# A long convolution by two-step Fourier transforms: length 4,096 split 64 by 32 in place of 128 by 16

## The chip, the core and the metric

The kernel runs on one core of a Trainium2 chip. The core has a matrix engine (TensorE, "PE" in the profile; its weight loads are "PEld"), VectorE (DVE), ScalarE (ACT), GpSimd (POOL) and SyncE (SP), which here issues all data transfers. Matmul results land in a separate memory, PSUM, and are copied ("evicted") to the on-chip memory SBUF by ScalarE or VectorE. The metric is the device time of one execution in microseconds; the median of three runs of the kernel before is 180.91 us (180.76 to 182.53).

## What is computed

Two independent results stand side by side in the output, for a sequence of 2,048 and 576 channels. A: keys `k` are filtered by a four-tap shift filter and multiplied by `v`; the product `kv` is convolved along the sequence with a filter `ssm_k` of 2,048 taps per channel; `kv` times a per-channel constant is added, and all is multiplied by `q`. B: a linear-attention block on `x`.

```python
# A
for t in range(ks):                                   # ks = 4
    k_shift = k_shift + k_pad[:, t:t + S, :] * shift_k[:, ks - 1 - t][None, None, :]
kv = k_shift * v
y_f = rfft(pad(kv, 2 * S)) * rfft(pad(ssm_k, 2 * S))  # shortened
y = irfft(y_f)[:S] + kv * ssm_D
a = q * y
# B, H = 32 heads of 18
phi = lambda t: jnp.where(t > 0, t + 1, jnp.exp(t)) + 1e-6
pq, pk = phi(q), phi(k)                               # q, k, v from x @ wqkv
kv = jnp.einsum("bhsd,bhse->bhde", pk, v)
num = jnp.einsum("bhqd,bhde->bhqe", pq, kv)
den = jnp.einsum("bhqd,bhd->bhq", pq, pk.sum(s)) + 1e-6
b = (num / den).reshape(B, S, D) @ wo
```

(`pad`, `rfft`, `irfft` and the last lines are shortened.)

## The kernel before, in words

The transform of the convolution is done with matmuls in two steps. Sequence position is written 16 a + b, with a on the 128 partitions and b from 0 to 15.

For each of five groups of channels (`ci`, four of 128 and one of 64) these units run; the number in brackets is the line of the profile:

- `hl`, `hT` [L445]: load the filter, 16 transposes put position a on partitions, one eviction of 2,048 columns, and the constant `ssm_D` is added to tap 0 on VectorE.
- `cv` 0 to 3 [L429 to L435]: the shift filter and the product with `v` on VectorE, in place in `v`.
- `h1`, `u1` (function `s1`) [L462]: first step, a matmul with the 128x128 table `G[ri][:, b, :]` for each b and real or imaginary part; four units for each group, each of eight matmuls into one PSUM tile and one eviction into `Ch` or `Cu`.
- `ht`, `ut` [L469]: two transposing transfers for each group (one for the last group) from `C` to `Ct`.
- `h2`, `u2` (function `s2`) [L485]: second step with the small table `W0` on tiles of 64 rows by 32 columns of the array, eight matmuls and one eviction for each unit, two units (x = 0, 1) for each half (`hf`), into `T` (filter) or `SU` (signal).
- `pX`, `pT` [L495, L497]: the products of the two spectra on VectorE.
- `i1` [L509]: inverse of the second step on 64-row tiles, 32 matmuls and one eviction into `V` for each unit, two units (z) for each half.
- `i2` [L522, L523]: inverse of the first step with `F`, the transposes of `G` (`FT`, L531); 16 matmuls and, on VectorE, the product with `q` straight from PSUM [L524].
- `st`: store.

Block B has the units `xT`, `xU` (transposes of `x`), `k` (16, L400), `q` (12, L409), `G` (5, L562), `kv`, `den`, `M` (L592), `bc` (L625), `o` (16, L634), each with one PSUM tile and one to two evictions or point operations.

The order of everything is written out by hand as a list of units (`ORDER`), one stream that every engine follows for its own part. A trailing `A` or `D` says whether ScalarE or VectorE evicts. PSUM is a ring of four tiles of two banks (`bufs=4`, tag `big`); every unit takes its tile from there in the order of the list. All transfers are issued on SP's queue, so one that waits holds up those behind it. The tables are made on the chip at the start: `io` and `iw` (GpSimd index patterns), `ix` (VectorE, index for the 128-point table), `iv` and `wk` (GpSimd: phases and a mask for the 16-point tables), `sin` and `sw` (ScalarE sines), `W` (VectorE), `id` (the identity for transposes), and `wu` (40 matmuls on zeros at the start).

Of the kernel before, what the change touches and what calls it, by code (L numbers as in the profile page):

```python
# [8 lines left out]
FP32 = mybir.dt.float32  # L9
BF = mybir.dt.bfloat16  # L10
# [6 lines left out]
S = 2048  # L17
# [13 lines left out]
wm io wu.0 wu.40 hl.0 xl.0 id ix.0 ix.1 xl.1 sin.1 ls hT.0.D one xT.0.D iw sin.0 FT.1.D iv wk xU.0.A lw.1  # L31
h1.0.0.0.A xT.1.D h1.0.0.1.D h1.0.1.1.D Wj sw W k.3 lw.0 xU.1.D kl.0 k.0 q.0.1 cv.0.0 h1.0.1.0.A q.1.2 xl.2
cv.0.1 hl.1 q.1.0 FT.0.A ht.0.1 cv.0.2 q.0.0 hT.1.A k.7 k.1 k.2 xl.3 h2.0.1.0.A hl.2 vl.0 cv.0.3 h1.1.0.0.A
k.6 h2.0.1.1.A q.1.1 ht.0.0 k.5 cv.1.0 u1.0.0.0.A k.4 u1.0.1.0.A u1.0.1.1.A xT.2.D u1.0.0.1.A h1.1.1.1.D q.0.2
h2.0.0.0.A xU.2.D ql.0 cv.1.1 h1.1.0.1.A xT.3.A h2.0.0.1.A cv.1.2 q.2.1 h1.1.1.0.A ut.0.0 cv.1.3 xU.3.A q.2.0
ut.0.1 u2.0.0.0.A u2.0.0.1.A hl.3 q.3.0 k.11 u2.0.1.0.A k.10 q.2.2 u2.0.1.1.A ht.1.0 h2.1.0.0.A hT.2.D
u1.1.0.0.D vl.2 ht.1.1 u1.1.1.0.A q.3.2 u1.1.1.1.A pX.0.1 u1.1.0.1.A h2.1.0.1.D k.12 h2.1.1.0.A k.14
h1.2.0.0.D h1.2.0.1.A k.9 kl.1 pT.0.1 h1.2.1.0.A h2.1.1.1.A cv.2.0 ut.1.1 k.15 k.8 ut.1.0 pX.0.0 u2.1.1.0.A
pT.0.0 vl.1 k.13 cv.2.1 h1.2.1.1.A u2.1.1.1.A q.3.1 eps kl.2 ht.2.1 u2.1.0.0.A cv.2.2 i1.0.0.0.A hc i1.0.0.1.A
i1.0.1.1.A lwv i1.0.1.0.A cv.2.3 G.2 h2.2.1.0.A cv.3.0 pX.1.1 u2.1.0.1.A cv.3.1 ht.2.0 h2.2.1.1.A hT.3.A G.1  # L40
u1.2.0.0.A hl.4 u1.2.0.1.A u1.2.1.0.D i2.0.1 es u1.2.1.1.A ut.2.0 pX.1.0 i2.0.0 h1.3.0.0.A cv.3.2 h1.3.1.0.A
G.3 pT.1.1 cv.3.3 h1.3.1.1.A h2.2.0.0.A cv.4.0 h2.2.0.1.A G.4 h1.3.0.1.A u2.2.0.0.A cv.4.1 ut.2.1 pT.1.0
cv.4.2 u2.2.0.1.A ht.3.0 G.0 lwo cv.4.3 i1.1.0.0.A u2.2.1.0.D u2.2.1.1.A i1.1.1.0.A i1.1.1.1.A pX.2.1 kv
ht.3.1 i1.1.0.1.A pX.2.0 pT.2.1 M.4 u1.3.0.0.A h2.3.0.0.A den u1.3.1.0.A u1.3.0.1.A h2.3.1.0.A i2.1.0
u1.3.1.1.A h2.3.1.1.A i2.1.1 u1.4.0.0.A u1.4.1.1.A M.3 bc.0.1 h2.3.0.1.A ql.2 ut.3.1 bc.0.0 bc.1.0 M.2
u1.4.0.1.A u1.4.1.0.A bc.3.0 M.1 M.0 ut.3.0 u2.3.1.0.A pT.2.0 hT.4.D u2.3.1.1.A bc.4.0 i1.2.0.0.A bc.2.0
ut.4.0 ql.1 i1.2.1.0.A i1.2.1.1.A u2.3.0.0.A u2.3.0.1.D pX.3.1 i1.2.0.1.A bc.3.1 h1.4.0.0.A o.5 bc.1.1 o.4
h1.4.0.1.A bc.2.1 bc.4.1 h1.4.1.0.A o.6 h1.4.1.1.D ht.4.0 i2.2.1 o.11 o.10 o.3 pT.3.1 o.13 pX.3.0 o.2 st.0
pT.3.0 h2.4.0.0.D u2.4.0.0.A u2.4.0.1.A i1.3.0.0.A i1.3.1.0.D i1.3.0.1.A h2.4.0.1.D pX.4.0 i1.3.1.1.D i2.2.0
o.12 pT.4.0 o.15 o.9 i2.3.0 o.1 i2.3.1 i1.4.0.0.D st.1 i1.4.0.1.A o.7 o.0 i2.4.1 i2.4.0 st.2 o.14 o.8  # L50
# [661 lines left out]
```

## Time and profile before

| | us |
|---|---|
| median of three runs | 180.91 |
| span of the profiled execution, first to last instruction | 178.8 |
| chain that ended last: PE 55%, DVE 24%, ACT 7%, POOL 5%, DMA 3% | |
| ACT waiting for `o_ps`, late in the run | 14.2 |
| DVE waiting for `i_ps` | 3.8 |

The rows of the groups that the change touches, with line, engine, operation, tensors, shapes and count, then busy us, mean ns of one, and idle time before them:

```
L462 PEld LDWEIGHTS <-G 128*128 128x128 bf16 x320 | 17.6, 98 | 2.7 <-issue 1.6
L509 PE MATMUL i_ps<-W,T 64*128 64x128 bf16 x288 | 16.9, 217 | 0.5 <-DVE pqT L393 0.5
L277 ACT ACTIVATE SU<-s_ps 128x1024 bf16<-128x1024 f32 x16 | 16.0, 1020 | 0.1
L277 ACT ACTIVATE Ch<-s_ps 128x1024 bf16<-128x1024 f32 x12 | 12.1, 1019 | 0.9 <-PE s_ps L462 0.9
L203 POOL TENSOR_SCALAR_AFFINE_SELECT sm<-sm 64x384 f32<-64x384 f32 x2 | 2.5, 1226 | 0.1
L218 ACT ACT_TABLE_LOAD x1 | 1.3, 1283 | 0.0
q8 instruction: 17, 0.28, 0.7%
```

A matmul's duration is its way through the array; matmuls follow each other more closely than that, so the spacing of their starts says what they cost. "64*32" is the used part of the array, rows by columns. The last row is the queue that brings instructions: packets, MB, share of 16 engines.

### The profile page before, as it was taken

How to read it: one execution, taken by the hardware profiler on the slowest of the kernel's cores; microseconds unless marked ns; L12 is line 12 of the kernel's file. 1: busy time of each engine (PE TensorE's matmuls, PEld its weight loads, DVE VectorE, ACT ScalarE, POOL GpSimd, SP SyncE). 2: the span in 40 equal slices, each digit the busy share in tenths (PEclk: the TensorE clock that was granted, in tenths of full speed). 3: DMA queues.
4: the chain of work that ended last, by engine and by line, in shares of the span. 5: the costliest groups of instructions: out<-in, count | busy, mean ns of one | idle time of the engine just before them, and what ended most of it. 6: DMA issues, size and time to landing. Idle time of an engine off the chain costs nothing.

```text
span 178.8 us, 5118 instructions
## 1 busy us (share of the span) xinstructions
PE 164.8 (92%) x2246; PEld 111.6 (62%) x2256; DVE 151.2 (85%) x174; ACT 128.7 (72%) x147; POOL 21.0 (12%) x59
## 2 busy tenths in 40 slices
PE   6996999999999999989799898998789999999991
PEld 6973575576654755575477453876557665686760
DVE  7987999999998879999949998779899789579720
ACT  3897578899998989984688257749887953754341
POOL 1189100000049810000000000000000000000000
PEclk9999999999999999999999999999999999999998
DMA  5999599973997799989722393791696937481295
GB/s 173 364 321 293 191 217 343 188 214 63 177 144 148 135 287 149 245 137 213 157 69 53 64 121 66 190 165 30 33 206 64 268 93 151 167 242 66 79 291 125
DMA packets 71208, 29.96 MB, mean 168 GB/s; under 512 B 46936, under 2 KB 70482, under 8 KB 71186
## 3 DMA queue, kind: packets, MB, share of 16 engines
q1 hardware_dynamic: 71186, 29.64, 74.0%
q8 instruction: 17, 0.28, 0.7%
q14 instruction: 5, 0.04, 0.1%
HBM read 15.48 MB, written 4.72 MB: 113 GB/s over the span
## 4 chain that ended last, share of the span: by engine, by line
PE 55%; DVE 24%; ACT 7%; POOL 5%; DMA 3%; issue 2%; SPq 1%; DVEq 0%; POOLq 0%; ACTq 0%
PE o_ps L634 11%; PE k_ps L400 7%; PE g_ps L562 7%; PE i_ps L509 6%; PE q_ps L409 6%; DVE at L432 5%; DVE at L431 5%; PE s_ps L462 5%; DMA x_sb<-in_B_x_dram 3%; PE bc_ps L625 3%; DVE pqT L393 3%; PE hT_ps L445 2%; PE s_ps L485 2%; ACT Cu L277 2%; DVE pk L393 2%
## 5 line engine op out<-in xcount | busy, mean ns | idle before, releaser
L409 PE MATMUL q_ps<-xT,wqk 128*126 128x512 bf16 (+3 forms) x100 | 23.7, 381 | 0.0
L400 PE MATMUL k_ps<-wqk,xT 128*128 128x64 bf16 (+3 forms) x154 | 21.5, 282 | 1.4 <-DVE Ch L279 0.8
L562 PE MATMUL g_ps<-pk,x_sb 128*128 128x65 bf16 (+3 forms) x156 | 20.4, 284 | 1.4 <-ACT wv_GT L566 1.1
L634 PE MATMUL o_ps<-wo_M,pqT 126*128 126x512 bf16 (+3 forms) x160 | 21.0, 286 | 0.0
L639 ACT ACTIVATE ob<-o_ps 128x576 bf16<-128x576 f32 x16 | 10.4, 652 | 14.2 <-PE o_ps L634 14.2
L462 PEld LDWEIGHTS <-G 128*128 128x128 bf16 x320 | 17.6, 98 | 2.7 <-issue 1.6
L400 PEld LDWEIGHTS <-xT 128*128 128x128 bf16 (+1 forms) x160 | 11.5, 97 | 12.3 <-issue 2.3
L277 ACT ACTIVATE V<-i_ps 128x1024 bf16<-128x1024 f32 x15 | 14.9, 1029 | 5.8 <-PE i_ps L509 5.8
L562 PEld LDWEIGHTS <-x_sb 128*128 128x128 bf16 (+1 forms) x160 | 11.0, 101 | 11.3 <-issue 1.9
L509 PE MATMUL i_ps<-W,T 64*128 64x128 bf16 x288 | 16.9, 217 | 0.5 <-DVE pqT L393 0.5
L409 PEld LDWEIGHTS <-wqk 128*126 128x126 bf16 (+3 forms) x100 | 12.4, 131 | 7.8 <-issue 1.1
L432 DVE TENSOR_TENSOR at<-at 128x2048 bf16<-128x2048 bf16 (+1 forms) x15 | 16.8, 1119 | 0.5
L634 PEld LDWEIGHTS <-pqT 126*128 126x128 bf16 (+1 forms) x160 | 10.9, 97 | 9.9
L509 PE MATMUL i_ps<-W,X 64*128 64x128 bf16 x288 | 16.8, 216 | 0.0
L431 DVE TENSOR_TENSOR at<-k,Wj 128x2048 bf16<-128x2048 bf16 (+1 forms) x15 | 16.7, 1111 | 0.1
L277 ACT ACTIVATE Cu<-s_ps 128x1024 bf16<-128x1024 f32 (+1 forms) x18 | 15.9, 928 | 0.7 <-PE s_ps L462 0.5
L277 ACT ACTIVATE SU<-s_ps 128x1024 bf16<-128x1024 f32 x16 | 16.0, 1020 | 0.1
L392 ACT ACTIVATE pqT<-q_ps,neg 126x1024 bf16<-126x1024 f32 (+1 forms) x12 | 11.6, 970 | 5.6 <-PE q_ps L409 5.6
L277 ACT ACTIVATE T<-s_ps 128x1024 bf16<-128x1024 f32 x15 | 15.3, 1026 | 0.0
L277 ACT ACTIVATE Ch<-s_ps 128x1024 bf16<-128x1024 f32 (+1 forms) x15 | 13.9, 937 | 1.1 <-PE s_ps L462 1.1
L524 DVE TENSOR_TENSOR q<-i_ps,q 128x1024 bf16<-128x1024 f32 (+1 forms) x10 | 11.0, 1109 | 4.0 <-PE i_ps L523 3.8
L392 ACT ACTIVATE pk<-k_ps,neg 128x576 bf16<-128x576 f32 x16 | 11.8, 742 | 2.6 <-PE k_ps L400 2.3
(121 smaller groups left out, 308.4 us busy)
## 6 DMA issues: line engine op xcount, KB each, us to landing
x_sb<-in_B_x_dram SPq DMA_DIRECT2D x4, 576.0 KB, 5.6
out_dram<-ob SPq DMA_DIRECT2D x16, 144.0 KB, 1.8
h_sb<-in_A_ssm_k_dram SPq DMA_DIRECT2D x4, 512.0 KB, 4.1
k<-in_A_k_dram SPq DMA_DIRECT2D x2, 1024.0 KB, 7.6
v<-in_A_v_dram SPq DMA_DIRECT2D x2, 1024.0 KB
q<-in_A_q_dram SPq DMA_DIRECT2D x2, 1024.0 KB
out_dram<-q SPq DMA_DIRECT2D x2, 1024.0 KB
wqk<-in_B_wqkv_dram SPq DMA_DIRECT2D x2, 576.0 KB, 8.9
```

What stands on the lines that cost most here:

```text
L277: nc.scalar.activation(out=out, in_=in_, func=ACT.Copy)
L392: nc.scalar.activation(out=out_ap, in_=ps_ap, func=ACT.Exp, bias=K.neg1[0:n, :])
L400: nc.tensor.matmul(ps[:, n0:n1], lhsT=xT[r // 4][0:fn, t, rr * 128:(rr + 1) * 128], rhs=wqk[0:fn, t, D + n0:D + n1], start=(t == 0), stop= ...
L409: nc.tensor.matmul(ps[0:hn, j, :], lhsT=wqk[0:fn, t, h0:h0 + hn], rhs=xT[g][0:fn, t, :], start=(t == 0), stop=(t == 4))
L431: nc.vector.tensor_tensor(out=t_, in0=kk[:, 3 - stage:19 - stage], in1=wb(stage), op=ALU.mult)
L432: nc.vector.tensor_tensor(out=a_, in0=a_, in1=t_, op=ALU.add)
L462: nc.tensor.matmul(ps[:, bi, 0:dc], lhsT=K.G[ri][:, b, :], rhs=xf(b), start=True, stop=True)
L509: nc.tensor.matmul(ps[:, r, g, :], lhsT=s[key, hf][64 * r:64 * r + 64, z, x, 128 * g:128 * g + 128], rhs=K.W[64 * r:64 * r + 64, m, :], st ...
L524: nc.vector.tensor_tensor(out=qs, in0=ps[:, :, 0:dc], in1=qs, op=ALU.mult)
L562: nc.tensor.matmul(ps[0:fn, n0:n1], lhsT=x_sb[:, r, f0:f0 + fn], rhs=pk[:, r, n0:n1], start=(r == 0), stop=(r == 15))
L634: nc.tensor.matmul(ps[:, n0:n1], lhsT=pqT[0:hn, c, r * 128:(r + 1) * 128], rhs=B['M'][0:hn, c, n0:n1], start=(c == 0), stop=(c == 4))
L639: nc.scalar.activation(out=ob, in_=ps[:, 0:D], func=ACT.Copy)
```

## The change

Position is now written 32 a + 16 h + b, with a from 0 to 63 and the half h on the two halves of the partitions, so the first step has 64 points and the second 32.

- First step: table `G` is 64 wide with real and imaginary parts side by side; two matmuls, one for each half of the partitions, on 64x128 tiles. A unit has four b and eight matmuls.
- Second step: 32x32 tiles, table `W` of 160 columns for everything small. One unit now does both x for a half: 64 matmuls, two PSUM tiles and two evictions (two letters, `AD`: the first by ScalarE, the second by VectorE).
- Inverse of the second step: 32x128 tiles, 128 matmuls of 64 columns, two PSUM tiles and two evictions for each half.
- Inverse of the first: 64x64 tiles, 64 matmuls of half the columns.
- `hT` and `FT`: 32 transposes of half the width in place of 16; `FT` also scales by 1/S.
- Small tables: index patterns by GpSimd in `io`, made together; `iv`, `wk`, `W` are gone. The index table has 1,024 columns in place of 2,048.
- Loads of `k`, `v`, `q` and the stores go by halves of the partitions.
- A new order of all units, with new letters. `sw` (sine of the small table, then setting the `Exp` table) now stands ahead of the two `sin`.
- Some tiles (`xT`, `wv_GT`, `wo_M`) are made at their first use, whichever unit that is.

```diff
+def _w32_index(tc, K):
     nc = tc.nc
     sm = K.sm
...
+    row = sm[:, 2:3].bitcast(I32)
+    nc.vector.tensor_single_scalar(out=row, in_=sm[:, 1:2].bitcast(I32), scalar=31, op=ALU.bitwise_and)
+    nc.vector.tensor_copy(out=sm[:, 3:4], in_=row)
+    K.wi = sm[:, 608:768].bitcast(I32)
+    nc.vector.scalar_tensor_tensor(out=K.wi, in0=sm[:, 288:448], scalar=sm[:, 3:4], in1=sm[:, 448:608], op0=ALU.mult,
+                                   op1=ALU.add)
+    nc.vector.tensor_single_scalar(out=K.wi, in_=K.wi, scalar=31, op=ALU.bitwise_and)
...
+def _sine32(tc, cpool, K):
...
+    K.W = cpool.tile([128, 160], BF, name="W32")
+    nc.scalar.activation(out=K.W[:], in_=K.wi, func=ACT.Sin, scale=TWO_PI / 32, bias=K.negpi[:])
     nc.scalar.activation(out=K.warm[:], in_=K.neg1[:], func=ACT.Exp)
...
-        hv = h[0:dc, :].rearrange("d (a b) -> d b a", b=16)
+        hv = h[0:dc, :].rearrange("d (a h b) -> d b h a", h=2, b=16)
         for b in range(16):
-            nc.tensor.transpose(out=ps[:, b, 0:dc], in_=hv[:, b, :], identity=K.ident[0:dc, 0:dc])
+            for g in range(2):
+                nc.tensor.transpose(out=ps[64 * g:64 * g + 64, b, 0:dc], in_=hv[:, b, g],
+                                    identity=K.ident[0:dc, 0:dc])
...
-        ps = psum.tile([128, 8, 128], FP32, name="s1_ps", tag="big")
-        for bi in range(8):
-            b = 8 * bg + bi
-            nc.tensor.matmul(ps[:, bi, 0:dc], lhsT=K.G[ri][:, b, :], rhs=xf(b), start=True, stop=True)
...
+        ps = psum.tile([128, 2, 4, 128], FP32, name="s1_ps", tag="big")
+        for bi in range(4):
+            b = 4 * bg + bi
+            for h in range(2):
+                nc.tensor.matmul(ps[:, h, bi, 0:dc].rearrange("p (f q y) -> p f q y", q=2, y=32),
+                                 lhsT=K.G[64 * h:64 * h + 64, b].rearrange("p r k -> p (r k)"),
+                                 rhs=xf(b)[64 * h:64 * h + 64].rearrange("p (q f y) -> p f q y", q=2, y=32),
+                                 start=True, stop=True)
+        evict(C[:, 0:dc, :].rearrange("p d (h g b) -> p g h d b", h=2, b=4)[:, bg],
+              ps[:, :, :, 0:dc].rearrange("p h b d -> p h d b"), eng)
...
-        ps = psum.tile([128, 2, 512], FP32, name="s2_ps", tag="big")
-        for r in range(2):
-            for j in range(2):
-                q = 32 * (2 * r + j)
-                for z in range(2):
-                    nc.tensor.matmul(ps[q:q + 32, z, :], lhsT=K.W0[64 * z:64 * z + 64, x, :],
-                                     rhs=Ct[64 * z:64 * z + 64, r, :, j, :], start=True, stop=True)
-        evict(s[dst, hf][:, :, x, :], ps[:], eng)
+        ps = [psum.tile([128, 2, 2, 256], FP32, name="s2_ps", tag="big") for _ in range(2)]
+        for x in range(2):
+            for r in range(2):
+                w = {(0, 0): 0, (1, 0): 32, (0, 1): 96, (1, 1): 0}[r, x]
+                for c in range(4):
+                    for t in range(4):
+                        nc.tensor.matmul(ps[t // 2][32 * c:32 * c + 32, t % 2, x, :],
+                                         lhsT=K.W[32 * t:32 * t + 32, w:w + 32],
+                                         rhs=Ct[32 * t:32 * t + 32, r, c], start=(r == 0), stop=(r == 1))
+        for i in range(2):
+            evict(o[:, 2 * i:2 * i + 2], ps[i][:], eng[i])
...
-        ps = psum.tile([128, 2, 4, 128], FP32, name="i1_ps", tag="big")
-        for g in range(4):
-            for n, (key, x, m) in enumerate((('T', 0, 0), ('T', 1, 1), ('X', 0, 2), ('X', 1, 2))):
-                for r in range(2):
-                    nc.tensor.matmul(ps[:, r, g, :], lhsT=s[key, hf][64 * r:64 * r + 64, z, x, 128 * g:128 * g + 128],
-                                     rhs=K.W[64 * r:64 * r + 64, m, :], start=(n == 0), stop=(n == 3))
...
+        ps = [psum.tile([128, 2, 8, 64], FP32, name="i1_ps", tag="big") for _ in range(2)]
+        for m in range(2):
+            for t in range(4):
+                for n, (key, x, w) in enumerate((('T', 0, 0), ('T', 1, 64), ('X', 0, 96), ('X', 1, 96))):
+                    for c in range(4):
+                        nc.tensor.matmul(ps[c // 2][:, c % 2, 4 * m + t, :],
+                                         lhsT=s[key, hf][32 * c:32 * c + 32, t, x, 128 * m:128 * m + 128],
+                                         rhs=K.W[32 * c:32 * c + 32, w:w + 64], start=(n == 0), stop=(n == 3))
+        for i in range(2):
+            d = 32 * hf + 16 * i
+            evict(V[:, :, d:d + 16], ps[i][:].rearrange("p c g j -> p j (c g)"), eng[i])
...
-            nc.tensor.matmul(ps[:, bi, 0:dc], lhsT=K.F[0][:, b, :], rhs=V[:, b, 0:dc], start=True, stop=False)
-            nc.tensor.matmul(ps[:, bi, 0:dc], lhsT=K.F[1][:, b, :], rhs=V[:, 16 + b, 0:dc], start=False, stop=True)
-        nc.vector.tensor_tensor(out=qs, in0=ps[:, :, 0:dc], in1=qs, op=ALU.mult)
+            for r in range(2):
+                for q in range(2):
+                    for h in range(2):
+                        nc.tensor.matmul(ps[64 * h:64 * h + 64, q, bi, 0:n],
+                                         lhsT=K.F[r][64 * q:64 * q + 64, 16 * h + b, :],
+                                         rhs=V[64 * q:64 * q + 64, 32 * r + 16 * h + b, 0:n],
+                                         start=(r == 0), stop=(r == 1))
...
+        for h in range(2):
+            nc.sync.dma_start(out=outA[h][:, :, d0:d0 + dn], in_=KV['q', gi][64 * h:64 * h + 64])
```

The new order begins and ends like this, the old one above it:

```diff
-wm io wu.0 wu.40 hl.0 xl.0 id ix.0 ix.1 xl.1 sin.1 ls hT.0.D one xT.0.D iw sin.0 FT.1.D iv wk xU.0.A lw.1
-h1.0.0.0.A xT.1.D h1.0.0.1.D h1.0.1.1.D Wj sw W k.3 lw.0 xU.1.D kl.0 k.0 q.0.1 cv.0.0 h1.0.1.0.A q.1.2 xl.2
...
-o.12 pT.4.0 o.15 o.9 i2.3.0 o.1 i2.3.1 i1.4.0.0.D st.1 i1.4.0.1.A o.7 o.0 i2.4.1 i2.4.0 st.2 o.14 o.8
+wm io wu.0 iw sw wu.40 ix.0 one xl.1 hc sin.1 ix.1 id sin.0 xT.1.D xU.1.D FT.0.D xl.0 xT.0.A xU.0.D lw.1 k.7 k.6
+lw.0 q.0.0 hl.0 q.0.2 hT.0.D ls Wj k.3 k.0 k.2 h1.0.3.A kl.0 cv.0.0 cv.0.1 h1.0.2.A k.1 q.0.1 xl.2 cv.0.2 xT.2.A
...
+o.12 o.11 pX.4.0 pT.4.0 i1.4.0.DA o.6 i2.4.0 i2.4.1 st.2 o.3 o.13
```

## The prediction

> **What bounds the kernel now.** First the page: the busy times of part 1, then the stretches by engine.
>
> ```profile
> PE 164.8 (92%) x2246; PEld 111.6 (62%) x2256; DVE 151.2 (85%) x174; ACT 128.7 (72%) x147; POOL 21.0 (12%) x59
> ```
>
> ```profile
> 0.00:20.00 20.00, 16.12 (x175) 13.55 (x177) 16.64 (x27) 13.65 (x13) 10.35 (x33) 1.00 0.98 297
> 20.00:60.00 40.00, 39.29 (x391) 25.23 (x393) 38.03 (x40) 35.49 (x39) 7.79 (x16) 1.00 0.80 172
> 140.00:179.00 39.00, 35.06 (x548) 23.15 (x542) 25.27 (x23) 19.00 (x27) 0.00 (x0) 0.98 0.58 163
> ```
>
> After length, the columns are PE, PEld, DVE, ACT, POOL. TensorE is the busiest engine throughout and VectorE is close to it until late. A busy PE is only overlapping durations, so I count its work by spacings. They come from the chain of waits (start, us, what) and the PE timeline (start, us, what):
>
> ```profile
> 38.61 0.90 PE s_ps L462 x16
> 57.63 0.56 PE s_ps L485 x16
> 141.64 1.23 PE o_ps L634 x10
> 26.18 1.00 PE hT_ps L445 x16
> ```
>
> ```profile
> 118.74 0.28 PE L509 MATMUL i_ps<-W,X 64*128 64x128 bf16 x4
> 118.85 0.28 PE L509 MATMUL i_ps<-W,T 64*128 64x128 bf16 x4
> 119.88 0.61 PE L462 MATMUL s_ps<-v,G 128*128 128x128 bf16 x8
> 120.43 0.41 PE L485 MATMUL s_ps<-Cth,W 64*32 64x512 bf16 x8
> 121.88 0.29 PE L604 MATMUL den_ps<-epsc,zsel 126*32 126x1 bf16 x20
> 122.10 1.07 PE L462 MATMUL s_ps<-v,G 128*128 128x128 bf16 x16
> ```
>
> The reader should see four prices. A full-array matmul of 128 columns takes 0.90/16 = 56 ns (L462). On half-array tiles (L509) four take 0.11 us: 28 ns each, two at once. On 64x32 tiles (L485) eight run at once, 16 of 512 columns in 0.56 us. A change of tile shape costs 0.10 us: eight of L462 at 56 ns from 119.88 end at 120.33, L485 starts at 120.43.
>
> So counted, with all other units by like rows (10 of `k` or `o` 1.23 us, 10 of `q` 2.17, a `G` 4.15), TensorE has 161 us of work in a span of 178.8. The other 17.4 are about 5 in the first 20 us (the units done by then add up to 15), 4 after the last matmul group (the last eviction and store), 8 of waits between. The median of the runs, 180.91, is 2.1 above the span; I carry that.
>
> **The change, part by part.**
>
> *Stage 1 (`h1`, `u1`).* 320 matmuls stay 320, on 64x128 tiles, two at once. Before: 256 of 128 columns at 56 ns and 64 of 64 columns at 29 (the 64-column matmuls of `o`: 1.23 less five of 217 leaves 0.15 for five) = 16.2 us. After: half, 8.1. Gain 8.1.
>
> *Stage 3 (`i1`).* Before 576 at 28 ns = 16.1. After 1,152 of 64 columns on 32x128 tiles, rounds of four on four row groups: 288 rounds. Nothing shows four row groups; the nearest row is the 64-column spacing, 29 ns for a round = 8.4. Gain 7.7; if only two overlap, 16.7 and a loss of 0.6. L604 bears on whether 64 columns are too few: its 20 one-column matmuls, in four column groups, take some 0.12 us (121.88 to 122.10 less the change of shape), 24 ns for four, so what a small matmul costs beyond its columns is paid by each tile beside the others. [...]
>
> *Stage 4 (`i2`).* Before 128 x 56 + 32 x 29 = 8.1. After 640 on 64x64 tiles, 160 rounds of four. I take 31 ns a round (64 weight columns load without the speed of the 128-column form: mean load 112 ns at 72 columns, 98 at 128) = 5.0. Gain 3.1; with two overlapping, a loss of 1.8.
>
> *Stage 2 (`h2`, `u2`).* 288 matmuls of 512 columns, eight at once, become 1,152 of 256 columns, sixteen at once: 36 rounds of 0.22 against 72 of 0.11. Nothing either way.
>
> *Transposes `hT`, `FT`.* 16 become 32 half as wide, in two column groups. The four column groups of L604 run together, so I cost this at nothing; if pairs don't overlap, 16 more at 62 ns (1.00/16) are 1.0 us for each of seven, 7 us.
>
> *Tile shapes.* Stages 1 and 4 and the transposes shared the full-array shape with `k`, `q`, `G`, `o`; now each has its own. Counted along the two orders the shape changes 99 times, 65 before: 34 x 0.10 = 3.4 us lost.
>
> TensorE: 161 - 8.1 - 7.7 - 3.1 + 3.4 = 146.
>
> *VectorE.* Evictions marked D: 15 fall to 8 (14 full ones to 7): -7 x 1.21 = -8.5. `FT` and `hT` +1 each, `xT` -2, all 1.2: nothing. Tables: before 7.6 (2.28, 1.23, 1.23, 0.70 for the index and 2.1 for the 16-point tables); after, 1,024 columns in place of 2,048 and one 160-wide table, about 4. Sum 151 - 12 = 139.
>
> *ScalarE.* +7 x 1.02 of evictions; `xT` +2, `hT` and `FT` -1 each (1.9) nothing; sines -2.4. The new order sets the `Exp` table between the sines, and a table load takes 1.28: two more, +2.6. Sum 129 + 7.4 = 136. The evictions of stages 1 and 3 now read PSUM in steps of 128 or 64 elements. `Ch` (pairs) at 1.019 and `SU` (plain) at 1.020 show no price for a pattern, so 1.02; 10% more would be 5 us.
>
> *Start.* The GpSimd tables behind `W` end the chain's first 18 us (select instructions of 1.2 us, then VectorE's 0.56), and PE idles some 2 us there. That goes. But the identity now stands behind the index tables on VectorE: GpSimd's iotas to about 2.7, tables 4, so the first transposes start near 6.9, and `FT.0` waits for the second sine: index to 6.5, two sines of 1.0, 8.6. PE reaches `k.7` near 10.7, against `k.3` at 12.1 with the transform of `h` behind it. By 10.7 it has done 7.3 us of work (the warm-up's 4.0 among it), so 3.5 are lost in front, 1.5 fewer than now; 2 more or fewer are possible.
>
> *Loads in halves.* `v`, `q` and the stores become two issues each, `k` stays at three; each SP issue took 0.3 to 0.6 us. The nine more add about 4 us on SP's queue, which waits some 80 us for transposes' inputs: nothing, and 1 us late per load where one is due just then.
>
> *Instruction supply.* PE's instructions grow from 4,514 to 8,578. The queue page has 17 instruction transfers for 17.6 blocks of 256, and each took 0.9 to 1.7 us. By the sums above seven new blocks (a whole `i1` is one) run in 0.9 to 1.3 us. I add 3 us.
>
> *Sum.* 146 + 3 + 3.5 + 4 = 156.5. VectorE (139) and ScalarE (136) now lie within 10 us of TensorE, so waits between will be no fewer than now; I take 8 as before. Span 164.5, time 167. A second way: I cut both orders into ten stretches and add, stretch by stretch, the busiest engine's work at the same prices: 170 us before, nine short of the span, and 152 after. 152 + 9 + 3 of instruction supply is 164.
>
> **The rivals.**
>
> *B, slower: TensorE's own instruction rate.* The sums need 128 instructions of `h2` in 0.45 us and 256 of `i1` in 0.93: 3.6 ns each. What the trace sustains is L509: eight in 0.11 us, 14 ns. L604 is faster, 40 in about 0.12 us, but they could have been queued behind 0.2-us matmuls. Sequencer and array stand apart: L592's wait is recorded at 118.93 and its matmul starts at 119.61, with 38 instructions between. With 38 in hand and 14 ns for the others, `h2`/`u2` lose 0.8 us x 18, `i1` 2.1 x 9, `i2` 0.76 x 10: 41 us, 208 in time. The 14 us between 167 and 181 are used up at 8 ns; mid-way, at 11, +28 gives 195. For it: nothing sustained below 14 ns is in the trace. Against: L509's 14 ns is what its 128 columns take on two tiles anyway, so it measures no limit of instructions. [...]
>
> *C, no change: PSUM evacuation.* `h2`, `u2` and `i1` now fill two of the four PSUM buffers at once and free neither until all is done: 0.45 or 0.93 us of matmuls, then two evictions of 1.02 on ScalarE. If each of the 27 units waits 0.6 us (half an eviction) for its second buffer, 16 us come back: about 181. For it: ScalarE is at 35.5 of 40 us from 20 to 60 already. Against: only 9 of these 27 follow another convolution unit directly on PE (36 of 54 before); most stand behind `k`, `q`, `G` or `o`, whose matmuls take longer than their evictions (1.23 against 0.74). [...]
>
> *D, faster still.* The waits between fall to nothing and the supply costs nothing: 146 + 3.5 + 4 + 2 = 155.5, up to 160.
>
> **How the numbers follow.** Forecast (160 to 176, around 167) 0.56; B (182 to 208, around 193, a little under mid-way) 0.24; C (176 to 184, around 180) 0.14; D 0.06. A percent, 179.1 to 182.7, is what a measurement of this kernel can tell from no change. Faster: forecast and D, and 0.05 of C: 0.67. Same: 0.07 of C and 0.01 of B: 0.08. Slower: 0.25. The range goes from 158, with half of D below, to 191, with somewhat over half of B above: 0.16 left out. The forecast's own range is 160 to 176.
>
> **What would show it.** Right: L462's successor spaced at 28 ns, a whole `i1` in about 0.95 us, a `h2` in about 0.5; TensorE's busy time down by some 15 us; VectorE near 139, ScalarE near 136. B: `i1` matmuls evenly spaced at 15 to 28 ns with no releaser, PEld idle put down to "issue". C: PE idle before `s_ps` or `i_ps` released by ScalarE, 10 us or more in sum. Wrong otherwise if the first `k` comes after 13 us, or if evictions of `C` or `V` are longer than 1.1 us.

## The result and the profile after

The changed kernel takes 212.78 us (median of 4 runs, 208.96 to 215.2) against 180.83 us for the kernel before on the same chip: ratio 1.159, 95% interval 1.150 to 1.169. Executions of one kernel fall into a faster and a slower state; the ratios and intervals here compare executions in the faster one, the medians are over all. The profiled execution took 211.94 us, its span is 210.1 us. First the page of the changed kernel: busy times, granted clock in 40 slices, two DMA queues, the shares of the chain that ended last.

```profile
PE 173.0 (82%) x4275; PEld 110.6 (53%) x4288; DVE 142.1 (68%) x164; ACT 136.7 (65%) x156; POOL 14.2 (7%) x39
...
PEclk9999999999999999859999997999985697979955
...
q1 hardware_dynamic: 71312, 29.64, 74.5%
q8 instruction: 33, 0.54, 1.1%
...
PE 59%; issue 14%; DVE 10%; DMA 9%; ACT 4%; SPq 3%; POOL 1%; ACTq 0%; POOLq 0%; DVEq 0%
```

VectorE and ScalarE stand where the sum put them (142 and 137 us; 139 and 136 were forecast). TensorE does not: its busy time rose by 8 us though its work was to fall by 15, and it stands idle more. The clock row has holes that the kernel before (the next row) lacks until its end, and "issue", time for which nothing in the profile is to blame, is now 14% of the chain; it was 2%.

```profile
PEclk9999999999999999999999999999999999999998
```

The changed kernel by stretches (length, then PE, PEld, DVE, ACT, POOL, granted clock, DMA share, GB/s):

```profile
0.00:20.00 20.00, 16.96 (x189) 13.12 (x192) 13.37 (x24) 15.60 (x16) 13.02 (x35) 1.00 0.85 239
20.00:60.00 40.00, 38.66 (x558) 24.40 (x563) 34.67 (x36) 34.10 (x39) 0.00 (x0) 1.00 0.98 161
...
140.00:180.00 40.00, 28.84 (x1037) 17.63 (x1036) 24.05 (x25) 24.69 (x33) 0.00 (x0) 0.83 0.68 123
```

Up to 60 us TensorE is as full as before. From 140 to 180 it is busy for 28.8 of 40 us at a mean clock of 0.83. What it waits for there is in the chain of waits (start, us, what), here over two units of `i1`, 256 matmuls:

```profile
150.28 0.80 PE i_ps L473 x86
151.08 3.97 issue
155.05 1.49 PE i_ps L473 x128
156.54 3.33 issue
159.88 0.77 PE i_ps L473 x39
160.65 4.91 PE o_ps L622 x20
```

TensorE breaks off in the middle of a unit, with every input there, stands for 4 us, runs 128 matmuls, and stands for 3.3 us. Counted in matmuls plus weight loads, the stops of more than 0.9 us (ten of them, later than 80 us) all lie at whole multiples of 256 from one another. Counted from one start to the next, the spacings over 0.3 us within two instructions of such a boundary add up to 27.9 us at 15 boundaries. The idle time in them is 24.2 us, at 11 boundaries; the kernel before has no idle gap over 0.3 us at one. The instruction queue (q8) has 33 transfers in place of 17. Its packets, of 16 KB each, show what ends the stops: each of the ten ends 1.3 to 1.5 us after such a packet has landed. In no trace here does a block of 256 start sooner than 1.1 us after its packet.

Behind seven of the ten stops come matmuls at half speed: `o` (L622) takes 4.91 us for 20 above, where the kernel before took 2.46. The records of the clock show 0.50 from 87.6 to 94.4 us, 128.5 to 131.9, 155.8 to 166.1, 172.9 to 176.3, 183.1 to 186.5 and from 200.2 to the end: 37.2 us, in 27.2 of which TensorE was busy.

The PE timeline between the stops (start, us, what) shows the prices of work that is not interrupted:

```profile
58.71 0.84 PE L445 MATMUL s_ps<-Ctu,W 32*32 32x256 bf16 x64
59.48 1.40 PE L353 MATMUL k_ps<-wqk,xT 128*128 128x512 bf16 x9
...
150.78 0.25 PE L473 MATMUL i_ps<-W,X 32*128 32x64 bf16 x8
150.85 0.23 PE L473 MATMUL i_ps<-W,T 32*128 32x64 bf16 x6
155.05 0.20 PE L473 MATMUL i_ps<-W,T 32*128 32x64 bf16 x2 [3.97 <-issue]
```

A `s2` of 64 has its successor 0.77 us after its start (0.45 and 0.10 for the change of shape were forecast), eight `i1` matmuls 0.06 to 0.07 us (8 ns each with their weight loads, four at once), up to the matmul where the block of instructions ends.

A ledger of the two profiled executions: TensorE busy 164.8 before and 173.0 after, its idle gaps 8.5 and 31.8. These 8.2 + 23.3 make 31.5 us; the spans differ by 31.2, since the idle time at start and end is 0.3 us shorter.

### The profile page after: what moved, and what is told of

The parts are those of the page before. It is cut to its first block, busy times and chain, and to the rows that moved or that the text cites. A ratio compares the mean times of both kernels' runs of the same rounds, so it can differ in the third digit from the quotient of the medians.

```text
span 210.1 us, 9157 instructions
## 1 busy us (share of the span) xinstructions
PE 173.0 (82%) x4275; PEld 110.6 (53%) x4288; DVE 142.1 (68%) x164; ACT 136.7 (65%) x156; POOL 14.2 (7%) x39
## 3 DMA queue, kind: packets, MB, share of 16 engines
q1 hardware_dynamic: 71312, 29.64, 74.5%
## 4 chain that ended last, share of the span: by engine, by line
PE 59%; issue 14%; DVE 10%; DMA 9%; ACT 4%; SPq 3%; POOL 1%; ACTq 0%; POOLq 0%; DVEq 0%
PE o_ps L622 11%; PE g_ps L548 10%; PE q_ps L362 6%; PE i_ps L473 6%; DMA x_sb<-in_B_x_dram 6%; PE k_ps L353 5%; PE s_ps L445 5%; PE s_ps L419 4%; PE hT_ps L399 4%; DMA wqk<-in_B_wqkv_dram 3%; PE i_ps L490 3%; SPq L319 2%; PE bc_ps L613 2%; ACT Cu L221 2%; DVE pqT L616 2%
## 5 line engine op out<-in xcount | busy, mean ns | idle before, releaser
L622 PE MATMUL o_ps<-wo_M,pqT 126*128 126x512 bf16 (+3 forms) x160 | 28.6, 344 | 0.0
L548 PE MATMUL g_ps<-pk,x_sb 128*128 128x65 bf16 (+3 forms) x156 | 22.4, 299 | 5.8 <-issue 5.7
L221 ACT ACTIVATE V<-i_ps 128x1024 bf16<-128x1024 f32 x14 | 13.8, 1024 | 13.7 <-PE i_ps L473 8.8
L221 ACT ACTIVATE Cu<-s_ps 128x1024 bf16<-128x1024 f32 (+1 forms) x19 | 17.3, 960 | 7.1 <-PE s_ps L419 3.6
L495 DVE TENSOR_TENSOR q<-i_ps,q 128x1024 bf16<-128x1024 f32 (+1 forms) x10 | 10.9, 1114 | 14.9 <-PE i_ps L490 14.8
L622 PEld LDWEIGHTS <-pqT 126*128 126x128 bf16 (+1 forms) x160 | 13.0, 113 | 15.1 <-issue 8.4
L221 ACT ACTIVATE SU<-s_ps 128x1024 bf16<-128x1024 f32 x18 | 17.4, 1023 | 2.7 <-PE s_ps L445 2.5
L473 PE MATMUL i_ps<-W,T 32*128 32x64 bf16 x576 | 11.8, 195 | 8.6 <-issue 8.4
L221 ACT ACTIVATE Ch<-s_ps 128x1024 bf16<-128x1024 f32 (+1 forms) x19 | 17.0, 936 | 0.2
L221 ACT ACTIVATE T<-s_ps 128x1024 bf16<-128x1024 f32 x16 | 15.6, 1024 | 1.5 <-PE s_ps L445 1.3
L346 DVE SCALAR_TENSOR_TENSOR pk<-pk,k_ps 128x576 bf16<-128x576 bf16 x16 | 11.9, 752 | 5.7 <-ACT pk L345 5.7
L419 PEld LDWEIGHTS <-G 64*128 64x128 bf16 x320 | 9.4, 95 | 11.7 <-issue 10.8
L552 ACT ACTIVATE wv_GT<-g_ps,ex 128x576 bf16<-128x576 f32 (+1 forms) x5 | 3.7, 739 | 17.7 <-DVE ex L551 17.7
L473 PEld LDWEIGHTS <-T 32*128 32x128 bf16 x576 | 10.1, 93 | 9.5 <-issue 9.0
```

Of the source, the lines that this page charges most:

```text
L221: nc.scalar.activation(out=out, in_=in_, func=ACT.Copy)
L346: nc.vector.scalar_tensor_tensor(out=out_ap, in0=out_ap, scalar=1.0, in1=ps_ap, op0=ALU.min, op1=ALU.max)
L419: nc.tensor.matmul(ps[:, h, bi, 0:dc].rearrange("p (f q y) -> p f q y", q=2, y=32), lhsT=K.G[64 * h:64 * h + 64, b].rearrange("p r k -> p ...
L473: nc.tensor.matmul(ps[c // 2][:, c % 2, 4 * m + t, :], lhsT=s[key, hf][32 * c:32 * c + 32, t, x, 128 * m:128 * m + 128], rhs=K.W[32 * c:32 ...
L495: nc.vector.tensor_tensor(out=qs, in0=ps[:, :, :, 0:n], in1=qs, op=ALU.mult)
L548: nc.tensor.matmul(ps[0:fn, n0:n1], lhsT=x_sb[:, r, f0:f0 + fn], rhs=pk[:, r, n0:n1], start=(r == 0), stop=(r == 15))
```

## The experiments

Theory 1: instructions reach TensorE in blocks of 256, with one block ahead, and a block that is used up faster than the next arrives stops the engine. Rivals: a cost added by each instruction; a lowest time of each instruction by itself, however dense (B's mechanism); no limit of instructions, but small tiles or late inputs. All edits are to the kernel before or to the changed kernel, as said.

| run | edit | median us | ratio to before, 95% |
|---|---|---|---|
| e1_dense | before, small matmuls halved | 198.75 | (195.63 to 200.22 us) |
| e2_wide | before, big matmuls quartered | 184.1 | 1.004 to 1.027 |
| e3_tail | before, 2,560 instructions behind its end | 212.52 | one run |
| e4_fewer | changed, `i1`, `i2` in fewer matmuls | 189.06 | 1.030 to 1.050 |
| e10_sum | changed, `i1` in 96 matmuls, not 128 | 202.2 | 1.094 to 1.116 |
| e12_sum_spaced | the same, `o` spread out | 205.07 | 1.115 to 1.135 |
| e9_pauses | before, two pauses of TensorE | 205.34 | 1.112 to 1.137 |
| e5_halves | before, transfers in halves | 184.62 | 1.006 to 1.015 |
| e6_whole | changed, transfers whole | 205.27 | 1.120 to 1.134 |
| e7_fewer_whole | changed, both of e4 and e6 | 182.13 | 0.998 to 1.008 |
| e11_flat | changed, `hT` reads adjacent columns | 207.19 | one run |
| e13_flat_too | e7 and e11 together | 181.06 | 0.993 to 1.002 |
| e14_early | e13, one transfer earlier | 180.61 | 0.987 to 0.998 |
| e8_sum | before, halves of X added first | 186.68 | 1.009 to 1.027 |

### More instructions in the kernel before: where it matters

The first run splits the matmuls of the short units, the second those of the long ones; both issue about 6,500 TensorE instructions in place of 4,514 for the same sums.

```diff
 # e1_dense: i1; the same in s2 (256 columns) and i2 (64)
+            for f in range(2):
...
-                    nc.tensor.matmul(ps[:, r, g, :], ..., rhs=K.W[64 * r:64 * r + 64, m, :], ...)
+                        nc.tensor.matmul(ps[:, r, g, 64 * f:64 * f + 64], ...,
+                                         rhs=K.W[64 * r:64 * r + 64, m, 64 * f:64 * f + 64], ...)
 # e2_wide: k; the same in q, G and o
-        for n0, n1 in ((0, 512), (512, 576)):
+        for n0, n1 in ((0, 128), (128, 256), (256, 384), (384, 512), (512, 576)):
```

> The kernel before, with the matmuls of its dense units cut in column halves: i1 and i2 into 64 columns, h2 and u2 into 256. Same sums, tiles, order and evictions; TensorE's instructions go from 4,514 to 6,498, the added ones where units are short. Theory 1 (instruction supply: a block of 256 instructions that runs in under some 4.4 us stalls TensorE until the next block is fetched): eight blocks then run in about 1.8 to 3 us, 19 us short in sum, of which two thirds show as in the changed kernel: 10 to 18 us with the slower clock after stalls, 191 to 200 us. Theory 2 (the new tile shapes or the new order are slow, not the count): array time grows by 1 to 3 us only, 181 to 184 us. Theory 3 (every instruction costs its time wherever it stands): 28 us for 4,064 more in the changed kernel is 7 ns each, so 1,984 more give 14 us, as the next run does.

> The kernel before, with the 512-column matmuls of k, q, G and o cut into four of 128: TensorE's instructions go to 6,554, nearly as many as in the run before, but the added ones stand in long units. Theory 1: only one block of 256 runs in under 4.4 us (3.8), so nothing stalls; the cut costs 2.3 ns for each of 1,020 matmuls, 2 to 3 us on TensorE: 182 to 185 us. Theory 2: the same, 182 to 185 us. Theory 3: 14 us and more, 195 us.

Nearly the same number of instructions costs 13 to 18 us in the short units (195.63 to 200.22 against 182.29 beside it) and 2 to 3 in the long ones (184.1). The waits of e1 (engine, line, what was waited for: us in total, times, longest):

```profile
PEld L511 <- issue: 8.0, 11, 1.9
PEld L568 <- issue: 6.2, 13, 2.6
PE i_ps L511 <- issue: 6.0, 5, 1.7
```

The longest wait on "issue" in e2 is 1.2 us, against 1.0 before. So it is not the number of instructions, but how many fall into a short time: a cost added by each instruction is out. A lowest time of each, B's mechanism, could give the same two results, for a quartered matmul of e2 takes 56 ns with its load (the price of L462's 128 columns), more than B's 28 for two instructions; the next run decides on that. The profiled execution of e1 also has 14.9 us at half clock, the kernel before 1.1.

### The price of a block alone

```diff
+    def small(n):
+        ps = psum.tile([128, 128], FP32, name="small_ps", tag="big")
+        for i in range(n):
+            j = i % 4
+            nc.tensor.matmul(ps[32 * j:32 * j + 32, 0:1], lhsT=K.ident[:, 0:32], rhs=K.ident[:, 0:1], ...)
...
-st.2 o.14 o.8
+st.2 o.14 o.8 sm.1280
```

> The kernel before, with 1,280 one-column matmuls on 32-column tiles added behind its last unit, where no data is loaded: ten blocks of 256 instructions whose array time is about 6 ns a pair, 0.8 us a block. Theory 1: bursts of 256 instructions with gaps at block boundaries, one block in 3 to 4.5 us, 30 to 45 us longer; if the fetch is slow only because of data transfers beside it, nearer 2.5 us a block. An even decode rate (rival B as first written) would show even spacing of 12 to 14 ns an instruction and 31 to 36 us. No limit: 8 us.

Ten blocks behind the last unit. The PE timeline of this run:

```profile
183.35 1.19 PE L659 MATMUL small_ps<-ident 128*32 128x1 bf16 x128 [2.54 <-issue]
186.81 1.18 PE L659 MATMUL small_ps<-ident 128*32 128x1 bf16 x128 [2.27 <-issue]
190.53 1.18 PE L659 MATMUL small_ps<-ident 128*32 128x1 bf16 x128 [2.54 <-issue]
193.99 1.18 PE L659 MATMUL small_ps<-ident 128*32 128x1 bf16 x128 [2.27 <-issue]
```

128 matmuls and their 128 loads run in 1.2 us (the granted clock is 0.50 there), and then TensorE waits for 2.3 to 2.5 although nothing else is left to transfer (DMA share 0.03). From block to block it is mostly 3.45 and 3.73 us in turn. In the changed kernel two blocks in a row at full clock are 3.73 us apart as well (entered at 119.4, 123.1 and 126.8 us). Not an even rate: bursts and one stop a block. The first 141 matmuls of the tail ran without a stop, over a boundary, and the next had to wait: one block stands ready ahead, no more.

The packets of q8 divide the time. In the tail, from its second stop on, a packet starts 1.0 to 1.3 us after a block is entered, takes 0.9 to 1.4 us, and the next block starts 1.2 to 1.4 us after it has landed. In the changed kernel the last part is nearly the same and the first is not: the packet starts from 0.2 us ahead of the entry to 4.6 us behind it, and the three longest stops (4.3, 4.0 and 3.3 us) stand where it started 2.4 to 4.3 us after. From entry to entry its ten stops have 2.3 to 6.6 us. What delays a packet's start is not shown.

### Fewer instructions in the changed kernel

```diff
 # e4_fewer: i1, 32 matmuls a unit in place of 128; i2 likewise 16 in place of 64
-                    for c in range(4):
-                        nc.tensor.matmul(ps[c // 2][:, c % 2, 4 * m + t, :],
-                                         lhsT=s[key, hf][32 * c:32 * c + 32, t, x, 128 * m:128 * m + 128],
-                                         rhs=K.W[32 * c:32 * c + 32, w:w + 64], ...)
+                    nc.tensor.matmul(ps[n // 2][:, n % 2, 4 * m + t, :],
+                                     lhsT=s[key, hf][:, t, x, 128 * m:128 * m + 128], rhs=K.W[:, w:w + 64], ...)
 # e10_sum: the halves of X added by VectorE, so i1 takes 96
+            nc.vector.tensor_tensor(out=X[:, :, 0, :], in0=X[:, :, 0, :], in1=X[:, :, 1, :], op=ALU.add)
...
-                for n, (key, x, w) in enumerate((('T', 0, 0), ('T', 1, 64), ('X', 0, 96), ('X', 1, 96))):
+                for n, (key, x, w) in enumerate((('T', 0, 0), ('T', 1, 64), ('X', 0, 96))):
 # e12_sum_spaced: e10, with the o units placed behind the densest units
-u2.3.1.AA i2.2.1 i2.2.0 u1.4.1.A
+u2.3.1.AA o.0 o.15 i2.2.1 i2.2.0 u1.4.1.A
```

> The changed kernel, with the 32-row tiles of i1 and the 64x64 tiles of i2 replaced by whole-array matmuls of the same columns that write the same PSUM regions: 32 in place of 128 and 16 in place of 64, at the same array time (a round of four tiles becomes one matmul). It leaves out the separation of the contraction by tiles, so the convolution's result is not computed. TensorE's instructions go from 8,578 to 5,890; evictions, order and widths of matmuls stay. Theory 1: nearly all fetch stalls go, and the half clock with them: 165 to 176 us. Theory 2 (order, evacuation of PSUM, start): only changes of tile shape are saved, 3 us and perhaps 5: 203 us or more. If the half clock comes from matmuls of 64 columns and not from stalls, the clock stays near 0.91 and the time is 180 to 190 us.

> The changed kernel with the two halves of X (x = 0 and 1, multiplied by the same table) added by VectorE behind the product, so that i1 issues 96 matmuls with 96 weight loads a unit in place of 128 and 128; same result. A model set up after the result: TensorE's instructions come in blocks of 256, and a block can start no sooner than 3.7 us after the block ahead of it was entered. Fed with the order and the unit times of the changed kernel it gives 29 us of stalls, where the trace has 28. With 192 instructions a unit it gives 23, and TensorE has 2 us less work: 201 to 206, against 212.8. If the stalls do not depend on the number of instructions, or VectorE's nine additions of 0.6 us come on the path: 210 to 215.

> As the run with the added halves of X, and 15 of the 16 output units o (20 matmuls in 1.34 us) moved in the order to behind the units with the most instructions. By the same model of blocks the stalls fall from 23 to 18 us: 196 to 202. If the spacing is without effect, as without it: 201 to 206.

The spacings at boundaries fall from 27.9 us to 2.3 in e4 (one stop), to 21.7 in e10 and to 17.5 in e12. The model of blocks, 3.7 us from one entry to the next, gives 29, 23 and 18 for the changed kernel, e10 and e12. So the stalls follow the blocks in size, not only in place. That holds for the sums; a single stop can be far from the model, which does not know when a packet starts. The stop left in e4 (2.05 us at 146.6) stands behind a block that ran for 5.7 us, and the packet for the next one started 4.9 us into it. By the ratios, e4 gains 21.5 us and e10 9.8, as forecast (6 fewer of stalls, 2 of matmuls, up to 1.8 of half clock). e12 is a miss: 4 us less of stalls, and a time 2% above that of e10 (ratios 1.125 and 1.105); its trace is already 3.6 us behind that of e10 at 43 us, ahead of every unit that was moved, with one more stretch at half clock at 32 us. No kernel of this form that computes the same came near the kernel before.

e4 was to reach 165 to 176 and stayed at 189. That lies in the range of the third forecast, half clock by matmuls of 64 columns, but the clock did not stay at 0.91 (0.94 to 0.96), and each of e4's stretches at half clock ahead of its end follows an idle stretch of 1.8 us or more. Its waits name the next thing that is late:

```profile
PE s_ps L419 <- ACT Ch L221: 4.8, 1, 4.8
ACT Ch L221 <- DMA Ctu<-Cu: 4.4, 1, 4.4
```

### The half clock

```diff
+    def pause(n):
+        nc.tensor.matmul(ps[:, 0:1], lhsT=K.ident[:], rhs=K.ident[:, 0:1], ...)
+        nc.scalar.activation(out=sc[:, 0, 0:1], in_=ps[:, 0:1], func=ACT.Copy)
+        for i in range(n):
+            nc.gpsimd.tensor_tensor(out=sc[:, 1 - i % 2, :], in0=sc[:, i % 2, :], in1=sc[:, i % 2, :], ...)
...
+        nc.tensor.matmul(ps[:, 0:1], lhsT=K.ident[:], rhs=sc[:, n % 2, 0:1], ...)
...
-u1.1.1.0.A q.3.2 u1.1.1.1.A
+u1.1.1.0.A q.3.2 pause.16 u1.1.1.1.A
...
-bc.0.0 bc.1.0 M.2
+bc.0.0 bc.1.0 pause.48 M.2
```

> The kernel before with two pauses put into TensorE's order, near 75 and near 125 us: a one-column matmul, a chain of 16 or 48 small dependent GpSimd operations behind it, and a one-column matmul that waits for the chain. At some 0.1 us an operation TensorE stands for about 2 and about 5.5 us. Theory H (an idle stretch of TensorE of some 2 us or more is itself followed by matmuls at half clock, whatever the instructions): a granted clock of 0.5 shows for 3 us or more behind the longer pause, perhaps behind the shorter, in a kernel that has none but at its end; the time rises by the pauses and by 1.5 to 4 us more, 189 to 194. Theory K (the half clock of the changed kernel comes from its small tiles or from instruction fetches): the clock stays at 1.00 and the time rises by no more than the pauses, 182 to 188.

An operation of the chain took 0.20 us, not 0.1, so TensorE stood for 6.8 us (63.3 to 70.1) and 13.6 (141.3 to 154.8). The stretches around both (columns as above):

```profile
64.00:70.00 6.00, 0.00 (x0) 0.10 (x1) 1.82 (x2) 0.03 (x1) 4.64 (x17) 0.82 0.77 202
70.00:75.00 5.00, 4.70 (x42) 2.83 (x42) 1.22 (x1) 1.97 (x3) 4.53 (x14) 0.53 0.16 32
141.00:155.00 14.00, 0.45 (x4) 0.29 (x3) 2.30 (x3) 0.39 (x2) 9.50 (x48) 0.57 0.26 54
155.00:163.00 8.00, 8.00 (x88) 5.09 (x89) 4.44 (x5) 4.80 (x7) 0.00 (x0) 0.50 0.15 29
163.00:180.00 17.00, 17.00 (x249) 10.60 (x246) 13.60 (x12) 10.30 (x15) 0.00 (x0) 0.99 0.63 155
```

Neither the changed kernel's tiles nor a late instruction is involved, and the clock is at 0.5 for 4.6 and 8.6 us after TensorE runs again: eight microseconds of full work at half speed behind the longer pause. The time rises by 22.9 us, 20.4 of them the pauses. Theory H holds for pauses of this length; one of 2 us was not made. In the changed kernel the stretches at half clock ahead of the last one are 3.4, 6.8 and 10.2 us long. As to what is enough to bring it on, e7 has a stretch at half clock from 120.9 to 127.7 us with no idle stretch near it longer than 1.82 us. In the traces of all runs every idle stretch of TensorE of 2.5 us or more lies in or is followed by half clock; of those from 1.3 to 2.5 us about two thirds are, and one of 2.45 us (e10, at 26.3 us) is not. What decides there is not shown.

### The transfers

```diff
 # e5_halves, in the kernel before: v, q, k and the stores
-        nc.sync.dma_start(out=t[:] if n == 16 else t, in_=src.rearrange("(a b) d -> a b d", b=16)[:, :, d0:d0 + dn])
+        for p in (slice(0, 64), slice(64, 128)):
+            nc.sync.dma_start(out=t[p], in_=src.rearrange("(a b) d -> a b d", b=16)[p, :, d0:d0 + dn])
 # e6_whole, in the changed kernel: the reverse; e7_fewer_whole: e6 and e4 together
```

> The kernel before, with only the loads of k, v and q and the stores of the first output made of two transfers each, over partitions 0 to 63 and 64 to 127 (rows, tiles, order and everything else unchanged). Theory L (a transfer over half of the partitions is itself slower): the 512-byte packets go from 31 ns to about 45, the DMA engines' summed time from 134 to some 155 us per engine, inputs come late from 20 to 60 us, time 183 to 189. Theory M (the halves cost only their issues, and the slower packets of the changed kernel come from something else, such as its interleaved rows or its other order): 512-byte packets stay at 30 to 33 ns, time 180 to 183.

> The changed kernel, with v and q loaded, and the first output stored, by one transfer over 128 partitions each, and k as in the kernel before. The rows then lie in natural order on the partitions, so the convolution that is computed is another one; the number and shape of all matmuls is as in the changed kernel. Theory L (halves are slow, and their lateness was part of the loss): DMA time per engine 159 to about 135 us, 512-byte packets at 31 ns, time 200 to 207, the gaps at every 256th PE instruction staying (20 to 30 us in sum). Theory M (the transfers are hidden anyway, all is instruction fetch): 209 to 213. A third: if the gaps themselves come from fetches that queue behind data packets, they shrink by half and time falls to 195 or lower.

> Both edits at once: the changed kernel with whole transfers, rows in natural order, and with i1 and i2 by whole-array matmuls of the same columns, 32 instead of 128 and 16 instead of 64 (the convolution is not computed). If late transfers were the rest of the miss: 170 to 178, with no wait of stage 1 on a transposed tile's DMA over 2 us. If the rest lies elsewhere (PSUM evictions, the order, the dearer transposes): 185 to 190 as with the fewer instructions alone.

The data queue of e5 and then of e6 (packets, MB, share of 16 engines over the span):

```profile
q1 hardware_dynamic: 71378, 29.64, 80.7%
```

```profile
q1 hardware_dynamic: 71186, 29.64, 65.2%
```

Share times span gives each engine's transfer time: 132 us before, 146 in e5, 157 in the changed kernel, 133 in e6, always for the same 29.64 MB. In the records the packets of 512 bytes, which are the rows of `k`, `v`, `q` and their stores, take 31 ns in the kernel before and in e6, 41.5 in e5, 45.6 in the changed kernel. A transfer over half of the partitions is slower by itself; whether the other 4 ns of the changed kernel come from its interleaved rows or its order is not shown. The trace shows the price of a half, not its reason.

In the kernel before, with slack on its queue, it costs 1.0% (0.6 to 1.5). In the changed kernel taking it away is worth 5.8 us by the ratios (205.27), and 6.9 beside the fewer instructions (182.13). e6 keeps most of the stops at the boundaries (23 us), and e3 has them with hardly any data moving (DMA share 0.03), so data packets in the way are not their main cause. Theory L's forecast for e7 fell: with stalls and halves gone it should have had 170 to 178. The other forecast, 185 to 190, missed too.

### What was left

```diff
 # e11_flat, in the changed kernel; e13_flat_too: the same on e7
-                nc.tensor.transpose(out=ps[64 * g:64 * g + 64, b, 0:dc], in_=hv[:, b, g],
+                nc.tensor.transpose(out=ps[64 * g:64 * g + 64, b, 0:dc], in_=h[0:dc, 128 * b + 64 * g:128 * b + 64 * g + 64],
 # e14_early: e13, and the transfer of u's second half ahead of the loads
-cv.3.0 u2.1.1.AA ql.0 i2.0.0
+cv.3.0 u2.1.1.AA ut.1.0 ql.0 i2.0.0
```

> The changed kernel with the 32 transposes of a hT unit reading 64 adjacent columns of h each, in place of every 32nd column; the filter's rows then stand in another order, so another convolution is computed. It tells why a unit of 32 takes 1.93 us (60 ns each, as long as one of 128 columns before, 62). If the two column groups do not overlap in this form: 1.8 to 2.0 us as now. If the reading of columns 64 bytes apart is what is slow: 0.9 to 1.1 us, as the 32 of FT (1.02 us).

The unit falls from 1.93 to 1.02 us. The two column groups do overlap (32 transposes in 1.02 us, where 16 of 128 columns took 1.00 before), and what is slow is fetching columns that lie 64 bytes apart. The groups of `hT`'s weight loads (its operand `h` is the one loaded; busy, mean ns, idle before) say it, in the changed kernel and then in e11:

```profile
L399 PEld LDWEIGHTS <-h_sb 128*64 128x64 bf16 (+1 forms) x160 | 9.7, 202 | 1.7 <-issue 1.3
```

```profile
L399 PEld LDWEIGHTS <-h_sb 128*64 128x64 bf16 (+1 forms) x160 | 4.5, 109 | 2.3 <-issue 2.0
```

Before, at 32 bytes apart, the same group has a mean of 154 ns. e11's time, 207.19, is a single run.

> The changed kernel with three things taken away at once: whole transfers, i1 and i2 by fewer whole-array matmuls, and hT's transposes reading adjacent columns (rows in natural or other order, the convolution not computed). The run with the first two had 182.1 us. hT's units fall from 1.93 to 1.02 us, 5 of them: if TensorE's work still sets the time, 4.6 us less, 176.5 to 179. If the late transposed tile near 90 us takes the gain back (it lands when its transfer lands, whatever TensorE does): 180 to 182.5.

> The same with one unit moved in the order: the transfer ut.1.0 (Cu to Ctu) ahead of the load of q and of two loads of h, which stood ahead of it on SP's queue. If that queue is what made TensorE stand 4.2 us near 92 us and run at half clock behind it: the wait goes, and 3 to 6 us with it, 171 to 176. If the wait only moves to the next late transfer (h, for hT.3, now behind it): no change, within 1.5 us of the run before.

Neither gave what was hoped: 181.06 and 180.61 us, 1.1 and 0.5 less, with intervals that overlap. In e13 TensorE is busy for 157.9 of 178.7 us (164.8 of 178.8 before), so there is 7 us less work in it, and no less time. The chain of waits of e14 names what it stands for:

```profile
85.02 7.41 DMA h_sb<-in_A_ssm_k_dram
...
144.00 6.87 DMA Ctu<-Cu
...
158.99 5.95 DMA Cth<-Ch
```

The transfer that was moved ahead no longer holds anything up; the load behind it, `h` for `hT.3`, does. The late part of the chain is a convolution group's own sequence of eviction, transposing transfer and stage 2, and no other work fills it, and the stops bring 17 us at half clock ahead of the end. Whether another order would close these gaps was not tried.

### A version that might have beaten both

```diff
 # e8_sum, in the kernel before
+            nc.gpsimd.tensor_tensor(out=X[:, :, 0, :], in0=X[:, :, 0, :], in1=X[:, :, 1, :], op=ALU.add)
...
-            for n, (key, x, m) in enumerate((('T', 0, 0), ('T', 1, 1), ('X', 0, 2), ('X', 1, 2))):
+            for n, (key, x, m) in enumerate((('T', 0, 0), ('T', 1, 1), ('X', 0, 2))):
```

> The kernel before, with the two halves of X (x = 0 and 1, which i1 multiplies by the same table) added by GpSimd ahead of i1, which then takes 48 instead of 64 matmuls a unit, 432 instead of 576 in all. If TensorE's work sets the time: 144 fewer at 28 ns, 4 us less work, time 176.5 to 179. If the waits between engines set it (GpSimd's add, 1 to 2.5 us for 1,024 columns, comes between the product and i1, or slows VectorE beside it): 180.5 to 184.

186.68 us, ratio 1.018 (1.009 to 1.027): slower, as in the second expectation, and above its range. Each addition takes GpSimd 2.1 us (median) between the product and `i1`; VectorE, with the same instructions as before, is busy for 156.5 us in place of 151.2, and TensorE's idle gaps grow from 8.5 us to 14.0. In the profiled execution (187.72 us) 10.2 us of TensorE's work also run at half clock, so it is busy for 166.2 us where 4 less than 164.8 were due. The work saved on TensorE is lost in waits and half clock. None of the kernels tried that do the whole computation is faster than the kernel before.

## Why the prediction was wrong

**The direction.** Forecast 167, measured 212.8; the slower case had 0.25. The step that failed first is "Instruction supply": "each took 0.9 to 1.7 us. By the sums above seven new blocks (a whole `i1` is one) run in 0.9 to 1.3 us. I add 3 us." I set the length of the transfer against the time of a block. The length was right (0.9 to 1.8 us after). What counts is the time from entering a block to the start of the next, with the wait ahead of the transfer and the 1.2 to 1.4 us behind it: 3.45 to 3.73 us alone (e3). At that price the term is 29 us by the model and 27.9 by the trace, not 3. The profile of before could not give 3.7, but it gave a bound: no block of 256 in it, counted at the boundaries of the stops, ran in less than 4.30 us, so every faster block was outside what was shown. In the trace after, twelve blocks hold less than 3 us of TensorE's work. Both ends (the packet's 0.9 and 4.30) belonged into the range.

**The half clock** was in no step. Up to 13.6 us (half of the 27.2 us of work done at half clock) come on top of the stops; e9 shows that a stop for another reason is followed by it too. So a stall's price was not its length alone. e4 against the changed kernel takes away stops and most of what followed them (10.3 us of work at half clock are left): 21.5 us by the ratios.

**"Loads in halves: nothing, 1 us late per load".** I priced the issues on SP's queue and not the packets: 24 us more for each DMA engine, 5.8 to 6.9 us in the time.

**"Waits between: 8 as before."** With stops, halves and dear transposes all taken away 181 us are left (e13), 14 more than 167. TensorE's idle gaps there are 13.9 us, and 14.7 us of its work run at half clock (up to 7.3 lost). The 8 itself was a fair reading of the profile before, whose idle gaps of TensorE are 8.5 us (the sum around it, 161 and 17.4, falls 0.4 short of the span). The trend was in the text (VectorE and ScalarE within 10 us of TensorE), and still 8 was carried. Shortening TensorE's work moved the bound to the chains between engines and transfers; by e13, which leaves out the convolution's result, the forecast would have missed without instruction fetch as well.

**TensorE's terms.** Right: stage 1 at half (27 ns a matmul); `FT` (1.02 us a unit, 0.89 before); `i1` 1.02 us for 0.93; `i2` 0.52 to 0.54 for 0.50. Mis-sized: stage 2, 0.67 us a unit less the change of shape for 0.45 (18 units, 4 us), and `hT`, 1.93 for 1.00 (5 units, 4.6 us). There the upper bound, "16 more at 62 ns", was the right value for another reason: not the column groups, but the distance of the columns read. With them the sum is about 155, not 146.

**The other steps** held: VectorE 142, ScalarE 137, evictions at 1.02 us in the new patterns, `xT` first at 6.98 us, `FT` at 8.44, the first `k` at 10.58 for 10.7.

**The rivals.** B had the right sign and a wrong mechanism, and 212.8 lies above its 208 too: there is no even 11 or 14 ns an instruction (`i1` runs at 8 ns a matmul with its load, four tiles at once, up to the block's end), but whole blocks. As it was stated it called for evenly spaced matmuls; they are absent, and e3 has bursts and stops. C asked for 10 us of TensorE idle released by ScalarE; the idle was released by "issue". D is out.

## What to carry over

Count the instructions of TensorE, matmuls and weight loads, in blocks of 256 along the order, and set each block's time against 3.7 us (blocks followed each other at 3.45 to 3.73 us in e3, at 3.73 in the changed kernel): where cutting the work into smaller tiles makes blocks shorter than that, expect a stop for the difference, and look in the trace at when the packets of the instruction queue start, for a late one stops a longer block too. Putting dense units between sparse ones took 4 us off the stops (e12), but not off the time. A stop of 2.5 us or more went with half clock in every trace here (ahead of the last stretch 3.4 to 10.2 us at a time in the changed kernel), and shorter ones often did; so it costs more than its length. And when the busiest engine's work is cut by a tenth, price the chain of transfers and evictions that is next, and the transfers' own shape, before carrying the old sum of waits.

## What the hardware showed unexpectedly

- In these traces a block of 256 TensorE instructions started no sooner than 1.1 us after its packet had landed, and a stop at a boundary ended 1.1 to 1.6 us after it. With a nearly idle DMA system (e3, DMA share 0.03) blocks followed each other at 3.45 to 3.73 us, and one block was ready ahead (the first 141 matmuls of the tail ran over a boundary without a stop).
- A transfer of 512-byte rows over partitions 0 to 63 or 64 to 127 took 41.5 ns a packet (e5), over all 128 31 ns (before), for the same bytes.
- Loading 64 columns of `h` into TensorE took 109 ns in the mean when they were adjacent (e11) and 202 ns when they were 64 bytes apart (the changed kernel).
- Sixteen tiles of 32x32 with 256 columns took 0.67 us for 64 matmuls in the changed kernel: 10.5 ns each, where twice the columns on eight tiles before gave 27.5 (0.22 us for eight).
